# Scores computed on quarters of the TensorE array, state products moved beside the outputs, and six load buffers in place of seven

## The chip, the cores and the metric

The kernel runs on one core of one Trainium2 chip. The metric is device time in microseconds (us) of one launch. The kernel before took 572.79 us (median of three runs, 572.37 to 572.82). One further execution was profiled: 576.07 us, of which the profile's span covers 574.3 us. All durations below come from that execution.

## The reference, cut to what matters

```
scores = (q @ k.T) / sqrt(64)                  # 8 batches, 8 heads, 576 positions, head size 64
ret    = scores * D    # D[i,j] = gamma_h**(i-j) for i >= j, else 0
x      = (ret @ v), heads side by side         # 4608 tokens x 512
expert = argmax over 8 of (normalised x @ normalised expert embedding)
gate   = softmax probability of that expert
out    = gate * (relu(x @ w1[expert]) @ w2[expert])
```

The first half is a decayed causal attention without a softmax ("retention"), the second a mixture of eight experts, each token going to one of them.

## The kernel before, in words

The 4608 tokens are 36 tiles of 128. A batch has 576 positions, four and a half tiles, so nine tiles (`KT`) make two batches, and in every tile with `t % KT == 4` one batch ends after 64 rows and the next begins. The retention stage takes the decay apart into a factor of the query position and one of the key position: keys and queries are multiplied as they are, values are scaled by `gneg` (`scale_v`, on GpSimd), and results are scaled by `gsb` (`emit_X`, on VectorE). Within a tile the masked product is computed directly; what earlier tiles of the batch contribute comes from a running state per head, the sum of key times value.

Per tile t, with the names that the prediction uses:

- `emit_A(t)`, the scores: for four head pairs p and both heads h, a matmul of 64 contraction rows gives all 128 keys by 128 queries, keys on the partitions. The two heads use the upper and lower 64 rows of the array and write two banks (`pa[0:2]` for even tiles, `pa[2:4]` for odd). VectorE then multiplies each bank by a 0/1 mask (`tri`, or `trix` where a batch boundary lies inside) into `pm`.
- `emit_QT(t)`: the earlier tiles' contribution, queries times the state `T` of tile t-1, eight matmuls on 64 by 64 quarters of the array.
- `emit_O(t)`: masked scores times values, accumulated with `emit_QT` in the bank pair `po`.
- `emit_U(t)`: the state's update, accumulated in the bank `pst`; ScalarE copies it out as `T`. Where `t % KT == 4` the values come from `vx`, a copy in which the rows of the batch that ended are zero. The last tile of a batch pair needs none.
- `emit_X(t)`, `emit_T(t)`: scaled result to SBUF, and four TensorE transposes to token rows. `emit_rows` copies them (ScalarE) and stores them to the DRAM tensor `xd`; `emit_sq` sums their squares.

The stage is written by hand as 18 steps `s` (the framework doesn't reorder it): step s works on tiles t = 2s and u = 2s+1, computes the scores of the next two tiles first, and transposes the two before. Routing is strewn between: logits (`route_logits`), one-hot ranks and a table of expert slots, in a rhythm of two steps. Each engine runs its instructions in the written order and waits on semaphores.

Loads are issued on SyncE's queue (SP) in written order: 512 KB of queries and keys (`qkt`) and 512 KB of keys and values (`kvt`; only the values, 256 KB, for the first four tiles, whose keys are transposed on TensorE by `turn_k`). Each of the two has `NLOAD` buffers. At the end of a step's products the loads of tiles t+7 and u+7 are written down as qk, kv, qk, kv; each waits until its buffer's last reader is done, and all behind it in the queue wait with it. The two stores of rows stand in the same queue.

After step 17 the first expert's matmuls begin (its first three token tiles are gathered from step 14 on), and from there the mixture stage runs to the end; the change doesn't touch it.

## Time and profile before

| | |
|---|---|
| median of three runs | 572.79 us |
| profiled execution | 576.07 us, span 574.3 us |
| TensorE matmuls (PE) | 559.5 us busy, 97% |
| weight loads (PEld) | 503.1 us, 88% |
| VectorE (DVE) | 404.2 us, 70% |
| ScalarE (ACT) | 352.1 us, 61% |
| GpSimd (POOL) | 207.7 us, 36% |
| DMA queue of the loads and stores (q1) | 53.5% of 16 engines' span |

Busy time is an average over a retention stage that lasts up to about 155 us and a mixture stage behind it. In the page's 40 slices the DMA engines stand at 9 tenths or more in the first nine slices and fall to between 0 and 9 tenths afterwards, while PE stands at 9 nearly throughout. A matmul's record has a modelled end that overlaps the next, so the time of a group on PE is read here from its start to the start of the next group.

### The profile page before, as it was taken

The numbers are of one execution on the slowest core, as the hardware profiler recorded it, in microseconds if no ns is written. First come the engines' busy times: TensorE is split into PE (matmuls) and PEld (weight loads), VectorE is DVE, ScalarE is ACT, GpSimd is POOL, SyncE is SP. The second block draws the span as 40 slices with busy tenths as digits, with TensorE's granted clock in tenths as the row PEclk, the third lists the DMA queues.
The fourth block names the chain that finished last, engine by engine and source line by source line (L and its number), as shares of the span: only waits on it lengthen the run. The fifth ranks groups of instructions, "written<-read, shape, count | busy, mean of one in ns | idle before, by whom it ended". The sixth has DMA issues, their size and how long they took to land.

```text
span 574.3 us, 13123 instructions
## 1 busy us (share of the span) xinstructions
PE 559.5 (97%) x5156; PEld 503.1 (88%) x5156; DVE 404.2 (70%) x880; ACT 352.1 (61%) x640; POOL 207.7 (36%) x188
## 2 busy tenths in 40 slices
PE   8999999998999999999999999999999999999995
PEld 7888888897898889988988998898799899889985
DVE  3677678786876696787798488579868847975400
ACT  1335545554565597577778678677877856876411
POOL 4582222225634418127306602630660462070021
PEclk8999999999999999999999999999999999999999
DMA  8999999997639556835915674593576559252011
GB/s 291 405 322 337 376 337 351 384 352 191 194 112 258 129 165 178 184 93 178 279 54 165 212 147 94 171 276 59 161 251 98 140 170 245 72 174 77 2 44 43
DMA packets 83067, 111.53 MB, mean 194 GB/s; under 512 B 48135, under 2 KB 48427, under 8 KB 82992
## 3 DMA queue, kind: packets, MB, share of 16 engines
q1 hardware_dynamic: 75312, 90.55, 53.5%
q0 software_dynamic: 7680, 19.95, 10.6%
q8 instruction: 51, 0.84, 0.6%
q14 instruction: 24, 0.20, 0.1%
HBM read 81.10 MB, written 19.94 MB: 176 GB/s over the span
## 4 chain that ended last, share of the span: by engine, by line
PE 75%; issue 11%; DVE 7%; ACT 3%; POOL 1%; DMA 1%; POOLq 0%; ACTq 0%; DVEq 0%; SPq 0%
PE pa L127 27%; PE po L127 22%; PE pst L127 15%; PE prow L127 8%; PE pa L131 2%; PE prow L131 1%; DMA graw<-graw 1%; DVE graw L454 1%; POOL out L1089 1%; ACT graw L419 1%; DVE w0f L993 1%; DVE pm L662 1%; DVE hs L1022 1%; DVE st L1035 1%; ACT w0f L990 1%
## 5 line engine op out<-in xcount | busy, mean ns | idle before, releaser
L1089 POOL DMA_INDIRECT out<-y,sid x40 | 42.8, 1070 | 231.4 <-ACT y L1085 220.5
L127 PE MATMUL po<-w2f,hs 128*128 128x512 f32 x408 | 94.1, 389 | 0.0
L127 PEld LDWEIGHTS po<-w2f,hs 128*128 128x128 f32 x408 | 76.4, 188 | 15.7
L127 PE MATMUL pst<-w2f,hs 128*128 128x512 f32 (+1 forms) x336 | 78.4, 382 | 0.0
L193 DVE TENSOR_TENSOR w2f<-wraw,w2f 128x1024 fp32r<-128x1024 f32 x32 | 39.4, 1230 | 50.4 <-ACT w2f L189 40.0
L127 PEld LDWEIGHTS pst<-w2f,hs 128*128 128x128 f32 x336 | 61.0, 188 | 11.4
L645 POOL TENSOR_TENSOR kvt<-kvt,cs 128x512 f32<-128x512 f32 x35 | 37.5, 1078 | 58.3 <-DMA kvt<-kv 49.5
L398 POOL DMA_INDIRECT gt<-gd,gid x40 | 51.0, 1274 | 18.0 <-issue 11.9
L419 ACT COPY graw<-graw 128x1024 uint16<-128x1024 uint16 x37 | 50.4, 1361 | 10.3 <-DMA graw<-graw 10.3
L127 PE MATMUL pa<-xxf,w0f 128*128 128x296 f32 (+2 forms) x348 | 50.8, 296 | 1.2 <-issue 1.2
L127 PEld LDWEIGHTS pa<-xxf,w0f 128*128 128x128 f32 x348 | 47.9, 188 | 1.8 <-issue 1.5
L662 DVE TENSOR_TENSOR pm<-pa,tri 128x512 f32<-128x512 f32 x64 | 40.1, 683 | 11.9 <-PE pa L127 11.7
L127 PE MATMUL prow<-w2f,hs 128*128 128x512 f32 x192 | 46.0, 389 | 0.0
L127 PE MATMUL pa<-qkt 64*128 64x128 f32 x576 | 43.1, 286 | 0.6 <-DVE bump L266 0.4
L127 PEld LDWEIGHTS prow<-w2f,hs 128*128 128x128 f32 x192 | 36.0, 188 | 7.5
L385 POOL DMA_INDIRECT graw<-xd,gid x26 | 32.7, 1259 | 24.8 <-DVE L_all L799 14.0
L127 PEld LDWEIGHTS pa<-qkt 64*128 64x128 f32 x576 | 38.4, 192 | 3.2 <-DVE bump L266 0.6
L464 ACT CAST xxf<-graw 128x128 fp32r<-128x128 f32 x70 | 31.8, 458 | 14.0 <-DVE graw L454 12.6
L127 PE MATMUL pa<-xsf,w0f 128*128 128x296 f32 (+2 forms) x240 | 39.9, 316 | 0.1
L454 DVE TENSOR_TENSOR graw<-graw 128x128 f32<-128x128 f32 x140 | 34.4, 287 | 6.0 <-ACT graw L419 4.8
L127 PEld LDWEIGHTS pa<-xsf,w0f 128*128 128x128 f32 x240 | 36.7, 189 | 0.9 <-issue 0.4
L127 PE MATMUL po<-pm,kvt 128*64 128x128 f32 (+1 forms) x640 | 35.3, 263 | 0.3 <-issue 0.3
(196 smaller groups left out, 1105.9 us busy)
## 6 DMA issues: line engine op xcount, KB each, us to landing
wraw<-w SPq DMA_DIRECT2D x64, 512.0 KB
qkt<-qk SPq DMA_DIRECT2D x36, 512.0 KB
kvt<-kv SPq DMA_DIRECT2D x32, 512.0 KB
xd<-xw SPq DMA_DIRECT2D x36, 256.0 KB
kvt<-kv SPq DMA_DIRECT2D x4, 256.0 KB
gt<-gd,gid POOLq DMA_INDIRECT x40
out<-y,sid POOLq DMA_INDIRECT x40
graw<-xd,gid POOLq DMA_INDIRECT x26
```

The lines of the kernel that those rows point to most:

```text
L127: pe[:] = [nc.tensor.matmul(*args, **kw)]
L131: pe[:] = [nc.tensor.transpose(*args, **kw)]
L193: nc.vector.tensor_tensor(out=self.to[:, 1, c * 1024 : (c + 1) * 1024], in0=self.raws.pop(c), in1=hi.bitcast(F32), op=ALU.subtract,)
L385: return nc.gpsimd.indirect_dma_start(out=t[:, :DM].bitcast(U16), out_offset=None, in_=xd[:rows, :], in_offset=bass.IndirectOffsetOnAxis(a ...
L398: nc.gpsimd.indirect_dma_start(out=g[:, i : i + 1], out_offset=None, in_=gd[:, :], in_offset=bass.IndirectOffsetOnAxis(ap=gid[:, a : a + 1 ...
L419: copy(t[:, :DM].bitcast(U16).rearrange("p (n h) -> p h n", h=2), t[:, XO : XO + DM].bitcast(U16).rearrange("p (h n) -> p h n", h=2),)
L454: nc.vector.tensor_tensor(out=v[:, 2 * k : 2 * k + 2], in0=a, in1=b, op=ALU.subtract)
L464: nc.scalar.copy(x[:, 0], u)
L645: eng.tensor_tensor(out=v, in0=v, in1=gneg[:, t % KT].unsqueeze(2).broadcast_to([P, H, D]), op=ALU.mult)
L662: nc.vector.tensor_tensor(out=pm[:, h], in0=banks[h].rearrange("p (c n) -> p c n", c=NP), in1=m.unsqueeze(1).broadcast_to([P, NP, P]), op= ...
L990: nc.scalar.copy(wop[n][:, 0], raw[n])
L1089: sc = nc.gpsimd.indirect_dma_start(out=out[:, :], out_offset=bass.IndirectOffsetOnAxis(ap=sid[:, a : a + 1], axis=0), in_=ys[i], in_offse ...
```

## The change

Seven edits, all in the retention stage:

1. `emit_A`: each score matmul of 128 keys becomes two of 64 keys, one for each half of the output partitions. The half whose keys come first in the tile gets all 128 queries, the other only the last 64 (its first 64 queries are masked anyway). For every second head pair the host stores keys and values with their two 64-row halves swapped, so which half of the array comes first alternates from pair to pair.
2. The masks get a version for swapped pairs; `vx` and the constants follow.
3. `emit_U(t + 2)` moves from behind the transposes to right behind `emit_O(u)`.
4. At the start, `emit_U(0)` moves behind `emit_A(1)` and `turn_k(1)`, and in step 0 `emit_O(0)` goes ahead of `emit_QT(1)`.
5. `NLOAD` is 6, and a step loads tiles t+6 and u+6.
6. The four loads are written where their buffers come free: qk behind `emit_QT`, kv behind `emit_O`.
7. The 40 warm-up matmuls write all four `pa` banks, since parts of them are no longer written by scores before the mask reads them.

```diff
-NLOAD = 7
+NLOAD = 6
...
-        warm = psm.tile([P, 512], F32, name="m")
-        for _ in range(NWARM):
-            mm(warm[:, :P], one, one, start=True, stop=True)
+        for i in range(NWARM):
+            mm(pa[i % 4][:, (i // 4) % 4 * P : ((i // 4) % 4 + 1) * P], one, one, start=True, stop=True)
...
             for p in range(NP):
-                for h in range(2):
-                    hs = slice(h * D, (h + 1) * D)
-                    mm(banks[h][:, p * P : (p + 1) * P], x[hs, p, 1, :], x[hs, p, 0, :], start=True, stop=True)
+                odd = p & 1
+                for o in (odd, 1 - odd):
+                    seen = slice(0 if o == odd else D, P)
+                    for h in range(2):
+                        hs = slice(h * D, (h + 1) * D)
+                        mm(
+                            banks[h][o * D : (o + 1) * D, p * P + seen.start : (p + 1) * P],
+                            x[hs, p, 1, o * D : (o + 1) * D],
+                            x[hs, p, 0, seen],
+                            start=True,
+                            stop=True,
+                            skip_group_check=True,
+                        )
...
         emit_A(0)
         turn_k(0)
         scale_v(0, nc.vector)
-        emit_U(0)
...
         turn_k(1)
+        emit_U(0)
...
-            emit_QT(t)
+            if s == 0:
+                emit_O(t)
+            else:
+                emit_QT(t)
+            load(load_qk, t + NLOAD)
             emit_QT(u)
+            load(load_qk, u + NLOAD)
             emit_U(u)
-            emit_O(t)
+            if s > 0:
+                emit_O(t)
+            load(load_kv, t + NLOAD)
             emit_O(u)
+            load(load_kv, u + NLOAD)
...
-            if s + 1 < HS:
-                loads(t + NLOAD)
-                loads(u + NLOAD)
+            emit_U(t + 2)
...
-            emit_U(t + 2)
             emit_X(t)
```

On TensorE, around the scores of tiles 0 and 1 (`pa_73` to `pa_76` are the four banks, with keys and queries from `qkt`; the last figures are output partitions by columns), before:

```order
L127 MATMUL pa_73<-qkt 128x128
L127 MATMUL pa_74<-qkt 128x128
L131 MATMUL prow<-ident,qkt 128x128 x4
L127 MATMUL pst<-kvt 64x64 x8
L127 MATMUL pa_75<-qkt 128x128
L127 MATMUL pa_76<-qkt 128x128
```

and after:

```order
L131 MATMUL pa_73<-qkt 64x128
L131 MATMUL pa_74<-qkt 64x128
L131 MATMUL pa_73<-qkt 64x64
L131 MATMUL pa_74<-qkt 64x64
L135 MATMUL prow<-ident,qkt 128x128 x4
L131 MATMUL pa_75<-qkt 64x128
L131 MATMUL pa_76<-qkt 64x128
L131 MATMUL pa_75<-qkt 64x64
L131 MATMUL pa_76<-qkt 64x64
```

A head pair is now four matmuls on four quarters, two of 128 and two of 64 columns, and the first state product (`pst`) no longer stands between the scores of tiles 0 and 1.

On TensorE in the second half of step 1 (`po` the outputs, `pst` the state, `pa_76` and `prow` the transposes), before:

```order
L127 MATMUL po<-qkt,T 64x128 x16
L127 MATMUL pst<-kvt 64x64 x8
L127 MATMUL po<-pm,kvt 64x128 x16
L131 MATMUL pa_76<-ident,xT 128x128 x4
L131 MATMUL prow<-ident,xT 128x128 x4
L127 MATMUL pst<-vx,kvt 64x64 x8
```

and after:

```order
L131 MATMUL po<-qkt,T 64x128 x16
L131 MATMUL pst<-kvt 64x64 x8
L131 MATMUL po<-pm,kvt 64x128 x16
L131 MATMUL pst<-vx,kvt 64x64 x8
L135 MATMUL pa_76<-ident,xT 128x128 x4
L135 MATMUL prow<-ident,xT 128x128 x4
```

The second state product has moved ahead of the transposes.

On SyncE's queue in step 2, before:

```order
L541 DMA qkt<-qk 128x1024
L548 DMA kvt<-kv 128x1024
L541 DMA qkt<-qk 128x1024
L548 DMA kvt<-kv 128x1024
L772 DMA xd<-xw 128x1024 x2
```

and after:

```order
L545 DMA qkt<-qk 128x1024 x2
L552 DMA kvt<-kv 128x1024 x2
L801 DMA xd<-xw 128x1024 x2
```

The step's second query-and-key load no longer stands behind its first key-and-value load.

## Rows read from the trace of the kernel before

**Rows 1.** Windows: length, busy time of PE, PEld, DVE, ACT, POOL; PE clock, DMA share, GB/s

```profile
50.00:60.00 10.00, 10.00 (x184) 8.74 (x172) 6.15 (x19) 5.47 (x12) 3.14 (x3) 1.00 1.03 402
70.00:90.00 20.00, 20.00 (x386) 17.89 (x386) 16.12 (x40) 10.18 (x21) 6.23 (x6) 1.00 0.96 340
110.00:130.00 20.00, 20.00 (x400) 17.95 (x400) 17.27 (x40) 10.55 (x22) 4.07 (x4) 1.00 1.01 360
```

**Rows 2.** Timeline of PE (start us, length us): scores begun in steps 7 and 15

```profile
69.46 2.32 PE L127 MATMUL pa<-qkt 64*128 64x128 f32 x32
...
133.04 0.48 PE L127 MATMUL pa<-qkt 64*128 64x128 f32 x2
```

**Rows 3.** Timeline of PE: the products of steps 3, 4 and 11

```profile
36.89 2.06 PE L127 MATMUL pa<-qkt 64*128 64x128 f32 x32
38.88 1.10 PE L127 MATMUL po<-qkt,T 64*64 64x128 f32 x32
39.91 0.69 PE L127 MATMUL pst<-kvt 128*64 128x64 f32 x16
40.42 1.92 PE L127 MATMUL po<-pm,kvt 128*64 128x128 f32 x32
...
46.20 0.67 PE L127 MATMUL po<-qkt,T 64*64 64x128 f32 x16
46.80 0.69 PE L127 MATMUL pst<-kvt 128*64 128x64 f32 x16
...
103.38 0.90 PE L127 MATMUL po<-qkt,T 64*64 64x64 f32 x32
104.21 0.69 PE L127 MATMUL pst<-kvt 128*64 128x64 f32 x16
```

**Rows 4.** Timeline of PE: transposes with and without a state product behind them

```profile
107.26 0.60 PE L131 MATMUL prow<-ident,xT 128*128 128x128 f32 x4
107.79 0.69 PE L127 MATMUL pst<-kvt 128*64 128x64 f32 x16
108.41 0.19 PE L127 MATMUL pa<-oh,stri 128*128 128x32 bf16 x1
...
115.86 0.60 PE L131 MATMUL prow<-ident,xT 128*128 128x128 f32 x4
116.30 0.31 PE L127 MATMUL pa<-st 128*128 128x80 bf16 x4
```

**Rows 5.** Timelines of DVE and PE: the start, to the scores of step 2

```profile
4.71 0.29 DVE L586 TENSOR_SCALAR tri<-cs 128x128 f32<-128x128 f32 x1 [3.37 <-DMA cs<-cst]
...
8.94 1.00 PE L127 MATMUL pst<-kvt 128*64 128x64 f32 x16 [1.81 <-DVE kvt L645]
9.88 2.08 PE L127 MATMUL pa<-qkt 64*128 64x128 f32 x16
...
19.94 2.06 PE L127 MATMUL pa<-qkt 64*128 64x128 f32 x32
...
28.23 1.94 PE L127 MATMUL pa<-qkt 64*128 64x128 f32 x30
```

**Rows 6.** Window of the first 16.5 us, columns as in Rows 1

```profile
0.00:16.50 16.50, 13.76 (x168) 12.37 (x170) 4.52 (x13) 3.20 (x5) 8.89 (x16) 0.90 0.86 307
```

**Rows 7.** Timelines of SP and POOL: issue of a load, and the scaling that waits for it

```profile
106.92 0.33 SPq L548 DMA_DIRECT2D kvt<-kv  x1
114.74 1.37 POOL L645 TENSOR_TENSOR kvt<-kvt,cs 128x512 f32<-128x512 f32 x1 [1.98 <-DMA kvt<-kv]
...
128.75 0.33 SPq L548 DMA_DIRECT2D kvt<-kv  x1
```

**Rows 8.** Timelines of POOL and PE: end of step 14, step 15, scores of step 16

```profile
134.22 1.22 POOL L385 DMA_INDIRECT graw<-xd,gid  x1 [13.96 <-DVE L_all L799]
138.01 4.06 POOL L645 TENSOR_TENSOR kvt<-kvt,cs 128x512 f32<-128x512 f32 x4
...
142.67 2.41 PE L127 MATMUL pa<-qkt 64*128 64x128 f32 x32
```

## The prediction

> **What bounds the kernel now.** I read the windows first, then the timeline of TensorE (PE) through a few steps, then the queues of SyncE (SP) and GpSimd (POOL). From 70 to 90 and from 110 to 130 us PE is busy for the whole window [rows 1]: matmuls stand back to back, so a step lasts as long as its matmuls. From the scores of step 7 to those of step 15 it is (133.04 - 69.46) / 8 = 7.95 us a step [rows 2]. Two others stand close behind. The DMA engines are at a share of 0.96 to 1.03 and move 340 to 402 GB/s [rows 1]. VectorE (DVE) is busy for 17.27 of 20 us [rows 1], which is 13.7 us in the 15.9 us of two steps. So what PE is spared is gained only until a load or the mask multiplications on DVE come late.

> **Scores on quarters.** Unstalled, the two tiles' scores of a step take 38.88 - 36.89 = 1.99 us from start to start, and the two tiles' QT products behind them 39.91 - 38.88 = 1.03 us [rows 3]: 3.02 together. No row shows the new score matmul in the new alternation, but QT is the same form (64 rows by 64 columns of the array, 128 or 64 moving columns), so I price by it. One tile of QT (16 records) takes 46.80 - 46.20 = 0.60 us, two take 1.03 [rows 3]; so 16 records of 128 columns cost 0.43 us and each run of this form 0.17 once. In step 11 one of the two tiles has 64 columns and both take 104.21 - 103.38 = 0.83 us [rows 3]; less 0.17 and 0.43 that is 0.23 us for 16 records of 64 columns. A tile's new scores are 16 records of each: 0.66 us. Scores and QT now have one form and stand in one run: 0.17 + 2 x 0.66 + 0.86 = 2.35 us, 0.67 less than before. Bounds: nothing saved, if four matmuls of unlike length don't overlap as four like ones do, or even a loss (rivals below).

> The 0.17 us at the head of a QT run [rows 3] now falls away between scores and QT. [...]

> **State product beside the outputs.** Behind the transposes it costs 107.79 - 107.26 = 0.53 for the transposes in front and 108.41 - 107.79 = 0.62 for itself, against 116.30 - 115.86 = 0.44 for the same transposes without one [rows 4]: 0.71. Between QT and O, products of the same kind as its new neighbours, it costs 40.42 - 39.91 = 0.51 [rows 3]. That saves 0.20 us a step. On ScalarE the copy of the state now stands ahead of both row copies, so the bank `prow` is read sooner; nothing waits for that.

> **A step.** 0.67 + 0.20 = 0.87 us off. I take back 0.17: even now the scores of step 7 take 2.32 and not 2.06 us, since they wait until VectorE and ScalarE have read the banks they overwrite [rows 2, 3], and about 0.9 us less matmul time now lies between the transposes into `pa[3]` and the scores of tile u+2 there. VectorE's 13.7 us for two steps still fit in 14.5. So 0.70 us a step (bounds 0.3 and 0.87), a step of 7.25 us; for steps 2 to 16, 15 x 0.70 = 10.5 us.

> **The start.** PE waits 1.81 us until the values of tile 0 are scaled on VectorE, and only then does the first state product run, with the scores of tile 1 behind it [rows 5]. Now the scores of tile 1 and their transposes fill this gap, and everything up to step 1 moves forward until the queries and keys of tile 5 hold it up. What is loaded up to them is 6 x 0.524 (qk) + 4 x 0.262 + 0.524 (kv) + 0.34 (constants) = 5.06 MB; 16.5 us at 307 GB/s are 5.07 MB [rows 6], so they land at about 16.5 us. Step 1 lasted 28.23 - 19.94 = 8.29 us [rows 5]; less 0.87, and less the 0.66 of tile 4's scores, which are done before, step 2 begins at 16.5 + 8.29 - 0.87 - 0.66 = 23.3 us. On VectorE the mask constants grow by about three instructions of 0.29 us [rows 5], and the masks of tiles 4 and 5 stand behind them: 24.2 us. That is 4.0 us ahead of 28.23 (bounds 1.5 and 5).

> **Six buffers, and where the loads are issued.** A load takes up to 114.74 - 106.92 = 7.8 us from issue to the scaling that waits for it [rows 7]. In the changed kernel a qk load issued behind QT(t) is needed by the scores two steps later, 2 x 7.25 - 1.6 = 12.9 us on; a kv load, issued 2 us later, by the state product at the end of that step. So one buffer less is not felt as such. The second qk load no longer waits in the queue behind the first kv, and the row stores behind all four wait no longer than before. What counts is the rate: a step moves 4 x 0.524 + 2 x 0.262 = 2.62 MB, in the four steps with an expert weight block 3.15 MB. At 402 GB/s [rows 1] that is 6.5 and 7.8 us against 7.25 us. The four long ones are 2.3 us over, the others have 0.7 us each to spare. I take a loss of 1.7 us (bounds 0 and 9; by the 402, since that window has stores and a weight block in it too).

> **POOL's queue in step 15.** The scaling of tiles 32 to 35 stands behind three gathers, which wait for the routing table: from 1.18 us after the step's first scores, the first scaling ends 138.01 + 1.02 - 133.04 = 6.0 us after them [rows 2, 8]. The state product of tile 32, moved forward, wants it about 1.9 (scores with their waits) + 0.8 + 0.5 + 1.9 = 5.1 us after them. PE, and all behind it, waits 0.8 us (bounds 0 and 1.5). In the kernel before, that product came behind the transposes and was covered.

> **Sum.** 4.0 + 10.5 - 1.7 - 0.8 = 12.0 us, against the profiled execution's 576.07 us (span 574.3 and 1.8 around it): 564.1. The median of the runs is 3.3 us lower, 572.79, so I expect 560.8 us. Everything behind step 17 hangs on the last rows and moves as a whole.

> **Rivals.**
> - *Loads become the bound.* For: a DMA share of 1.01 at only 360 GB/s, 0.96 at 340 [rows 1]. Against: 402 at 1.03. Up to the last load 36 x 0.524 (qk) + 34 x 0.524 (kv) + 30 x 0.262 (stores) + 4 x 0.524 (weights) + 0.34 = 47.0 MB move, 41.9 of them after 16.5 us. At 350 GB/s the last lands at 16.5 + 119.7 = 136.2 us, and the scores of tiles 34 and 35, at 142.67 before [rows 8], start then: 6.5 us, and 0.5 in the rest: 565.8 us (563 at 360, 569 at 340 GB/s). The last kv was issued at 128.75 [rows 7], so even this leaves a gain: PE didn't need it so early.
> - *Quarters in lockstep.* A group of four goes only when its longest is through: 16 groups of 0.43 / 4 = 0.1075 us are 1.72 us for two tiles, the run 2.75, the step 0.27 + 0.20 - 0.17 = 0.30 us shorter. 15 x 0.30 + 3.6 - 0.8 = 7.3 us: 565.5. No row has lengths that alternate; the order of halves, turned from pair to pair, speaks against it, as the half with 64 columns is the next pair's first. [...]
> - *VectorE becomes the bound.* Its 13.7 us for two steps need 0.8 us of waits to reach 14.5. For: in every second step masks, one-hots and the weight split stand in one chain. Against: it waits for PE between them. With half the gain, 0.35 us a step, and 0.6 us for loads, 5.3 + 4.0 - 0.8 - 0.6 = 7.9: 564.9 us.
> - *Slower: only two quarters run at a time.* Then a tile's scores are the eight pairs of before (0.91 us) and eight of half the length (0.45): 2.72 us for two tiles, and the run 0.17 + 2.72 + 0.86 = 3.75, 0.73 longer. A step grows by 0.73 - 0.20 + 0.17 = 0.70, 15 x 0.70 = 10.5; the start keeps 1.3, POOL's wait stays: 572.8 + 10.5 - 1.3 + 0.8 = 582.8 us. It decides from a pair of scores of 2.3 us on. Against it: QT already runs its 16 records in 0.43 us, half of what the wide form takes.

> **How the numbers follow.** Forecast 0.48; loads 0.18; lockstep 0.17; VectorE 0.10; two at a time 0.07. The forecast's own range is 557 to 564 us. Loads, lockstep and VectorE lie between 563 and 569, so 556 to 568 us leaves out the slower case, the slowest loads and a step that loses its full 0.87: under 2 in 10. Faster by over 0.2% (about what a measurement of this kernel can tell from no change): 0.91; within it 0.02; slower 0.07.

> **What would show it.** In the profile of the changed kernel: scores of two tiles in 1.3 to 1.6 us from start to start (1.7 or more is lockstep, 2.3 or more two at a time), QT right behind; a state product of 0.51 us behind the outputs; scores of step 2 at 24 us; steps 7 to 15 at 7.2 to 7.3 us on average; a PE wait of under 1 us for scaled values in step 15. Idle time of PE before scores that ends with `qkt`'s landing would show the loads as the bound, waits for `pm` before the outputs VectorE. The prediction is wrong if the step has its shorter scores and the mixture stage still doesn't begin 10 us or more sooner.

## The result: 4.1 us slower, not 12 us faster, and the profile after

The changed kernel takes 575.76 us (median of 14 runs, 572.81 to 578.97), the kernel before 571.63 us beside it (14 runs, 570.52 to 573.38): ratio 1.0064, 95% interval 1.0044 to 1.0084. The forecast was 560.8 us, with a range of 556 to 568. Both profiled executions took 576.07 us. That is the changed kernel's median, but some 4 us above that of the kernel before; a second profile of each was taken later.

Windows of the changed kernel, columns as in [rows 1]:

```profile
16.50:30.00 13.50, 10.28 (x206) 9.73 (x209) 7.83 (x19) 2.89 (x7) 6.63 (x11) 0.75 0.88 321
70.00:90.00 20.00, 17.45 (x455) 15.51 (x448) 15.98 (x40) 10.73 (x23) 5.35 (x5) 1.00 0.97 343
110.00:130.00 20.00, 18.47 (x463) 16.25 (x463) 18.38 (x43) 12.43 (x25) 5.12 (x6) 1.00 0.96 360
```

TensorE was busy for the whole of two of these windows [rows 1]; now it is idle for 1.5 to 2.6 us of each 20, and DMA share and GB/s are about what they were. In the first window the granted clock is at its lower level (0.5 in the profile's rows, against 1.0) from 19.06 to 25.89 us; it fell while TensorE waited 3.22 us, until 20.49, for the queries and keys of tile 5. The matmuls did become shorter. This is the PE timeline of a step of the changed kernel without a stop, to the next scores, and the same step of the kernel before:

```profile
77.91 2.00 PE L131 MATMUL pa<-qkt 64*64 64x128 f32 x60
79.69 0.27 PE L131 MATMUL po<-qkt,T 64*64 64x128 f32 x1
79.73 0.29 PE L131 MATMUL pa<-qkt 64*64 64x64 f32 x4
79.81 1.09 PE L131 MATMUL po<-qkt,T 64*64 64x128 f32 x31
80.82 1.97 PE L131 MATMUL po<-pm,kvt 128*64 128x128 f32 x32
82.62 0.63 PE L131 MATMUL pst<-kvt 128*64 128x64 f32 x16
83.18 1.08 PE L131 MATMUL pa<-xT,E 128*32 128x128 f32 x32
...
85.50 0.43 PE L131 MATMUL pa<-qkt 64*64 64x128 f32 x2
```

```profile
76.98 2.41 PE L127 MATMUL pa<-qkt 64*128 64x128 f32 x32
...
85.30 0.87 PE L127 MATMUL pa<-qkt 64*128 64x128 f32 x8
```

7.59 us against 8.32: 0.73 less, where 0.70 was forecast. The state product takes 83.18 - 82.62 = 0.56 us. But such a step is the exception. PE's waits from 14 to 150 us (total, times, longest), the changed kernel and then the one before:

```profile
PE po L131 <- issue: 5.3, 6, 1.5
PE pa L131 <- DMA qkt<-qk: 3.2, 1, 3.2
PE pa L131 <- DVE tab L359: 2.4, 3, 1.1
PE pa L131 <- DVE t L299: 1.4, 2, 1.0
PE pa L131 <- issue: 0.9, 3, 0.5
PE pst L131 <- issue: 0.9, 1, 0.9
```

```profile
PE pa L127 <- issue: 0.9, 1, 0.9
PE po L127 <- issue: 0.9, 3, 0.4
```

"issue" is a wait for nothing that the profile names, in the middle of a run of equal products. One of them, in PE's timeline, and the DMA queues in the 0.2 us from 71.1 to 71.3 us:

```profile
71.10 0.76 PE L131 MATMUL po<-qkt,T 64*64 64x128 f32 x18
73.36 0.66 PE L131 MATMUL po<-qkt,T 64*64 64x128 f32 x13 [1.50 <-issue]
```

```profile
q8 instruction: 1, 0.02, 30.0%
```

A packet of the instruction queue starts there, and 2.2 us later TensorE goes on. The pages' rows of that queue for the whole execution, after and before, say how large a packet is:

```profile
q8 instruction: 55, 0.90, 0.6%
```

```profile
q8 instruction: 51, 0.84, 0.6%
```

The traces have 14308 instructions of all engines after and 13123 before; over 55 and 51 packets that is 260 and 257 each, in 16 KB. Between stops on TensorE lie one or more times 256 matmuls and weight loads. The windows from stop to stop in the changed kernel (34.16, 39.92; 90.60, 97.25; 107.80, 113.78):

```profile
34.16:39.92 5.76, 5.40 (x127) 4.48 (x127) 3.35 (x10) 3.42 (x7) 4.88 (x8) 1.00 0.93 320
90.60:97.25 6.65, 5.54 (x129) 4.91 (x129) 4.38 (x13) 4.25 (x8) 1.32 (x2) 1.00 0.97 357
107.80:113.78 5.98, 5.43 (x128) 4.80 (x129) 3.55 (x11) 3.47 (x8) 0.00 (x0) 1.00 0.96 339
```

From the records, a block's packet starts 0.5 to 4.7 us after TensorE has entered the block ahead of it (2.7 on average from 14 to 150 us; 2.4 in the kernel before), and its instructions run 2.2 us after that at the earliest. Before, 256 instructions lasted 6.8 us on average, so the next block was there in time but for two stops of over 0.3 us (1.8 us together). Now they last 5.8, and of 23 blocks 11 came late, by 10.0 us together. A step has 363 instructions instead of 299 (recorded matmuls and weight loads of steps 7 and 8, halved), so it uses up 1.42 blocks instead of 1.17. Without their stops 256 of them would last 5.77 - 10.0 / 23 = 5.3 us on average, and a packet that starts later than 5.3 - 2.2 = 3.1 us into the block ahead makes TensorE wait (an estimate from these means; single blocks differ). A step is now (143.27 - 29.36) / 14 = 8.14 us between the scores of steps 2 and 16, where 7.25 was forecast.

### The profile page after: what moved, and what is told of

It reads as the page before. It is cut to its first block, busy times and chain, and to the rows that moved or that the text cites. A ratio compares the mean times of both kernels' runs of the same rounds, so it can differ in the third digit from the quotient of the medians.

```text
span 574.3 us, 14308 instructions
## 1 busy us (share of the span) xinstructions
PE 548.4 (95%) x5732; PEld 495.1 (86%) x5732; DVE 409.2 (71%) x882; ACT 354.6 (62%) x640; POOL 209.2 (36%) x192
## 3 DMA queue, kind: packets, MB, share of 16 engines
q0 software_dynamic: 7680, 19.95, 10.5%
HBM read 81.10 MB, written 19.94 MB: 176 GB/s over the span
## 4 chain that ended last, share of the span: by engine, by line
PE 64%; issue 13%; DVE 11%; DMA 5%; ACT 3%; POOL 2%; SPq 0%; POOLq 0%; ACTq 0%; DVEq 0%
PE pa L131 23%; PE po L131 18%; PE pst L131 14%; PE prow L131 7%; DMA qkt<-qk 3%; DVE graw L458 2%; PE pa L135 1%; DMA graw<-graw 1%; DVE pm L691 1%; POOL out L1122 1%; DVE w0f L1026 1%; DMA graw<-xd,gid 1%; DVE xT L779 1%; DVE hs L1055 1%; PE prow L135 1%
## 5 line engine op out<-in xcount | busy, mean ns | idle before, releaser
L402 POOL DMA_INDIRECT gt<-gd,gid x40 | 50.4, 1260 | 19.4 <-issue 11.9
L773 ACT COPY T<-pst 128x256 f32<-128x256 f32 x32 | 11.9, 373 | 60.3 <-PE pst L131 60.1
L131 PE MATMUL pa<-qkt 64*64 64x64 f32 (+1 forms) x1152 | 37.2, 254 | 9.6 <-DMA qkt<-qk 4.3
L131 PEld LDWEIGHTS pa<-qkt 64*64 64x64 f32 x1152 | 29.8, 136 | 15.7 <-DVE entry L613 3.3
L468 ACT CAST xxf<-graw 128x128 fp32r<-128x128 f32 x70 | 31.7, 458 | 13.7 <-DVE graw L458 13.4
L131 PE MATMUL po<-pm,kvt 128*64 128x128 f32 (+1 forms) x640 | 37.0, 266 | 2.7 <-issue 2.7
```

What stands on the lines that cost most here:

```text
L131: pe[:] = [nc.tensor.matmul(*args, **kw)]
L402: nc.gpsimd.indirect_dma_start(out=g[:, i : i + 1], out_offset=None, in_=gd[:, :], in_offset=bass.IndirectOffsetOnAxis(ap=gid[:, a : a + 1 ...
L468: nc.scalar.copy(x[:, 0], u)
L773: nc.scalar.copy(T, u[:, :NP])
```

## The experiments

Theory A: TensorE's instructions arrive too late. Theory B: VectorE frees the score banks too late. Theory C: six buffers, the loads' new places or the new start cost it. "Block-end stops" below are those of 0.3 us or more between 14 and 150 us, from the start of a block's last instruction to the start of the next block's first; so they are longer than the idle times in the lists of waits, and a wait for another engine at such a place is in them too. The start of the mixture stage is that of its first product on TensorE: 155.59 and 154.20 us in two profiles of the kernel before, 156.25 and 161.37 of the changed one. Each ratio is to runs of the kernel before on the same chip; times and profiles of different runs are mostly of different chips, on which the kernel before takes 571.0 to 575.0 us.

**Each part alone, on the kernel before.**

```
e1_quarters: emit_A on quarters, with the masks, gneg and the inputs' layout that go with it
e1_loads:    NLOAD = 6; load_qk(t+6) behind emit_QT(t), load_kv(t+6) behind emit_O(t)
e1_start:    emit_U(0) behind turn_k(1); in step 0 emit_O(t) in place of emit_QT(t)
e1_state:    emit_U(t + 2) behind emit_O(u), ahead of emit_T
```

> The kernel before with the scores on quarters alone (seven buffers, loads, start and state product as before). Theory A, TensorE's instruction supply: the quarters add 32 matmuls and 32 weight loads a step, and the run of them stops for the next block of instructions; gaps without a semaphore of 0.5 to 1.8 us stand 1 to 2 us behind the 16 KB packets of the instruction queue, some 5 to 9 us in all up to 150 us, so of the 10 us that shorter matmuls spare at most half is left: 567 to 571 us against 571.6. Theory B, VectorE comes late for the score banks: the gaps before scores are 0.7 to 1.3 us in the even steps, 4 to 5 us in all: 566 to 568. Theory C, the six buffers and the new places of the loads cost it: here they are as before, so the whole 0.67 us a step shows, 561 to 563.

> The kernel before with six load buffers and each load handed out where one comes free, nothing else. Theories A and B: no change, within 1 us of before. Theory C: 5 us or more slower, with waits of TensorE for qkt and a second fall of its clock.

> The kernel before with the order of the first two tiles changed alone (scores and transposes of tile 1 ahead of the first state product, outputs of tile 0 without the QT product). By the prediction: up to 4 us faster at the scores of step 2. If tile 5's queries and keys are what the start waits for, as the trace of the changed kernel shows (they landed at 20.4 us and TensorE waited 3.2 us and then ran at half clock): within 1.5 us of before.

> The kernel before with the state product moved beside the outputs alone. By its price in the trace, 0.20 us a step: 3 us faster. Theory B: it stands ahead of the transposes, so these and all that VectorE does with them come 0.5 us later; 0 to 1 us faster. Theory A says the same as the price: 3 us.

Measured: quarters 579.93 us (ratio 1.0134, 1.0092 to 1.0176), loads 571.38 (0.9978 to 1.0017), start 571.13 (0.9966 to 1.0003), state product 567.08 (0.9923, 0.9896 to 0.995). So the slow part is the one whose matmuls became shorter, and C is out as the cause. A was nearest for the quarters, though its 567 to 571 us were 9 us too low: the block-end stops are 16.7 us where 5 to 9 were expected, and after two of them (to 50.02 and 68.02 us) the granted clock falls to its lower level for 3.4 us each (0.76 on average from 48 to 55 us, 0.74 from 66 to 72.5). The longest stop, in the PE timeline of the quarters alone, 2.3 us behind a packet:

```profile
107.81 0.46 PE L131 MATMUL po<-pm,kvt 128*64 128x64 f32 x9
110.76 1.51 PE L131 MATMUL po<-pm,kvt 128*64 128x64 f32 x34 [2.49 <-issue]
```

**Same instructions, less traffic, and the control without quarters.**

```
 def load_qk(t):
+    if t >= NLOAD:
+        qkt[t] = qkt[t - NLOAD]
+        return
```

> The changed kernel without the loads of queries and keys from tile 6 on (the buffers of the first six tiles are read again, so the scores are those of other tiles): same instructions on every engine, 1.05 MB a step less to load. Theory A, TensorE runs dry at the end of each 256 instructions, since the next 16 KB of them start 3 to 4 us late behind the loads and are usable 2.2 us after that: the packets start within 1.5 us of the last block's end, the gaps at the block ends (9.4 us from 14 to 150 us in the changed kernel) shrink under 2 us, and the time falls by 6 to 9 us to 567 to 570. Theory B, VectorE late for the score banks (0.7 to 1.3 us in front of scores in even steps): gaps there as before, time within 2 us of the changed kernel's 575.8. Theory C, loads late by themselves: as A for the time, but the gaps that vanish are those that end with a landing of qkt, of which the changed kernel has one only, at 20.5 us.

> The changed kernel without quarters (568.3) and without the loads of queries and keys from tile 6 on, as in the half-traffic run (scores of other tiles). With quarters that gave 9.1 us. Theory A: TensorE has 299 instructions a step here and rarely runs dry (2.5 us of block-end gaps with the full traffic), so less traffic gives 1 to 3 us: 565 to 567, and both half-traffic kernels come out alike or the one with quarters (566.7) ahead. If less traffic helps by other ways (VectorE, the start, row stores): 5 us or more here too, 560 to 563.

Measured: with quarters 566.71 us (0.988 to 0.9921), 9.1 us below the changed kernel; without, 574.26 where before is 574.95 (0.9967 to 1.0021), against 0.994 with the full traffic. The totals hold more than the loop: behind the first mixture product these two take 421.7 and 423.8 us to the end, all others 416 to 419; that the other scores change the routing is likely, but wasn't tried. In the loop itself the answer is plain. The mixture stage begins, with quarters, at 143.99 instead of 156.25 and 161.37 us, and without them at 148.59 instead of 149.32. The 148.59 hold some 1.7 us of the short stops that are told last in this document, in step 15; from the scores of step 2 to those of step 15 it is 97.5 instead of 106.1 and 110.7 us with quarters, and 100.7 instead of 102.9 without. So the kernel without quarters gains 2.2 us, which is what its block-end stops took, and the one with quarters 8.6 and 13.2, of which its stops make 6.7 and 10.1. The packets' mean delay falls from 2.7 to 1.6 us with quarters and from 2.4 to 0.6 without, the block-end stops from 10.0 to 4.0 (A had said under 2) and from 2.2 to 0. PE's waits of the half-traffic run with quarters:

```profile
PE po L131 <- issue: 1.8, 3, 0.8
PE pa L131 <- DVE tab L359: 1.2, 3, 0.5
PE pa L131 <- DVE t L299: 1.0, 1, 1.0
```

Theory A is shown: same instructions, earlier packets, fewer stops, and no more gain in the control than its own stops. Of B some 2 us stay: in front of scores TensorE waits 2.6 us for VectorE here, and 4.7 with the full traffic.

**More instructions without shorter work.**

```
-for h in range(2):
-    mm(banks[h][:, p*P:(p+1)*P], x[hs, p, 1, :], x[hs, p, 0, :], ...)
+for o in range(2):
+    for h in range(2):
+        mm(banks[h][:, p*P+o*D : p*P+(o+1)*D], x[hs, p, 1, :], x[hs, p, 0, o*D:(o+1)*D], ...)
```

> The kernel before with each score matmul cut in two of 64 moving columns each, on the same 64 by 128 form: as many matmuls and weight loads more as the quarters bring (32 and 32 a step in the records), the same work for the array, nothing left out. Theory A: the blocks of 256 instructions are used up sooner than they arrive, gaps without a semaphore at their ends of 8 us or more from 14 to 150 us, and the time at least 8 us above 571.6, that is 580 or more, even if the halves cost no more on the array. Theory B: nothing but what the halves cost on the array; gaps at the block ends stay at 2 us, 571 to 574.

Measured: 606.39 us (ratio 1.0621), with a single stop at a block's end, of 0.3 us. A's number is met for a reason that neither theory had: a product of half the columns took as long as one of all of them.

```profile
82.35 4.05 PE L127 MATMUL pa<-qkt 64*128 64x64 f32 x64
86.33 1.10 PE L127 MATMUL po<-qkt,T 64*64 64x128 f32 x32
```

3.98 us for 64 of these, 1.99 for 32 of twice the columns [rows 3]. Each product brings a weight load of its own (1152 of each in the trace); whether that or the product sets the time wasn't tried. With the scores' time doubled, a block lasts long enough (6.8 us on average) for the next one to arrive. As a test of A this is void.

**The other parts without quarters; the weight split moved.**

```
e2_no_quarters: the changed kernel with emit_A, masks and rows as before
e2_split_late:  at((8 + 2*i, 1), ...) -> at((9 + 2*i, 1), ...)
```

> The changed kernel with the scores on the whole width as before (state product beside the outputs, start and loads as changed). The three other parts alone gave 4.6, 0.5 and 0.3 us. Theory A: their sum, 566 to 567. Theory C (the six buffers and the start cost when the step is shorter): 570 or more, with the 3.2 us wait for tile 5 at the start.

> The changed kernel with the first weight split of the loop (high and low half on VectorE and ScalarE) moved from the even steps to the odd ones, away from the routing. Theory B: the waits of 0.7 to 1.3 us in front of scores in steps 6, 10 and 14 fall to 0.3, and the time by 3 to 4 us to 572. Theory A: TensorE then reaches the end of a block sooner and waits there instead; the time within 1.5 us of 575.8.

Measured: without quarters 568.28 us (0.9924 to 0.9956), 1 to 2 us short of the gain that the sum had; with the split moved 580.03 (1.0134 to 1.0192). There B predicted 572 and A 574.3 to 577.3, and both missed. The waits that were meant did go: in front of the scores of steps 5, 9 and 13 (6, 10 and 14 as the expectation counts) the changed kernel has 0.5, 1.05 and 0.99 us, and this one none over 0.2. But TensorE, spared them, stops at the next block's end: 14.8 us of these instead of 10.0. And at 146.5 us a new wait for VectorE of 4.5 us came, about as long as this kernel is slower than the changed one. So sparing TensorE those waits gained nothing, as A said; the new wait is the edit's own.

**Fewer buffers, other loads.**

```
e3_five_buffers:   NLOAD = 6 -> 5
e3_quarters_state: e1_quarters with e1_state, seven buffers
e3_start_state:    e1_start with e1_state, seven buffers
```

> The changed kernel with five load buffers: fewer loads stand in the DMA queues at once. If the instruction packets' delay (2.7 us on average in the changed kernel, 1.6 with half the traffic) goes with what is queued ahead of them, it falls to 2 us or less and the time to 570 or below, unless loads then come late for the scores (waits for qkt, 580 or more). If it goes with the share of the DMA engines' time, which stays at 0.93 to 0.98, no change: within 2 us of 575.8.

> The changed kernel with seven buffers, the loads where they were and the old start: quarters and state product alone. If the handed-out loads help the instruction packets through (delay 3.1 us on average with quarters alone, 2.7 in the changed kernel): above 575.8, 576 to 579, with more than 9.4 us of gaps at the block ends. If the six buffers and the start cost the changed kernel anything: below 574.

> The kernel before with the state product beside the outputs and the new order of the start, seven buffers and loads as before. If the parts add up: 571.6 - 4.6 - 0.5 = 566.5. It and the state product alone (567.1) are what the versions with quarters must beat.

Measured, in this order: 582.81 us (1.0172 to 1.0227), 575.27 (1.0057 to 1.0117) and 567.38 (0.9918 to 0.9964). With five buffers the packets are as late as before (2.75 us) and loads come late too: PE waits 8.8 us for qkt, 6.7 of them at once. With quarters and seven buffers the stops are 12.6 us, and the time falls into neither of the two expected ranges. Buffers and order of the loads decide little there; the two good parts without quarters don't add beyond the state product alone.

**Quarters for one tile of the two.**

```
 for p in range(NP):    # e3_one_tile: quarters if t is even; e4_second_tile: if t is odd
     mm(banks[h][:, p*P:(p+1)*P], x[hs, p, 1, :], x[hs, p, 0, :], ...)   # the other tile
```

> The changed kernel with only the first tile of each step on quarters; the second tile's scores run on the whole width with the same layout and masks. Theory A: a step has 331 instructions on TensorE instead of 363, at 5.6 us for 256 (the mean of the blocks of the changed kernel from 14 to 150 us is 5.77, of the half-traffic run 5.27) 7.25 us, under the 7.4 us that its matmuls take; so the block ends stop being the bound, the gaps there fall from 9.4 to 3 to 5 us, and half of the quarters' 10 us is left: 563 to 566. If every added instruction costs in proportion instead: between no quarters (568.3) and all (575.8), 572. Theory B: the waits for VectorE stay, 570 to 573.

> The changed kernel with only the second tile of each step on quarters (the first tile's scores wide). With the first tile alone on quarters the scores of a step took 2.18 and 2.30 us, against 2.25 and 2.34 with none: the second tile's scores wait there until ScalarE has squared the rows in bank 3 and VectorE has read bank 1. If these reads set the start of the second tile's scores, quarters in the second tile shorten the step by 0.33 to 0.38 us, and 331 instructions a step still arrive in time: scores in 1.9 to 2.0 us, block-end gaps of 2 to 4 us, 563 to 565. If what counts is the number of instructions alone: as with the first tile, 570.

> The same with seven buffers and the loads where they were (start and state product as changed; without quarters this gave 567.4). Same gain of 0.33 to 0.38 us a step: 562 to 564; with more delay of the instruction packets than with the loads handed out (3.1 against 2.7 us with all scores on quarters), 564 to 567.

Measured: 570.11 us (0.9971 to 1.0026), 568.17 (0.9922 to 0.9967) and 569.16 (0.9944 to 0.9998). None is better than no quarters at all. The gains that were expected of A's reasoning were missed in all three; only the first lies in a stated range, at the edge of theory B's 570 to 573. The stops are down, to 1.8 us with the first tile on quarters and 4.6 with the second, but the gain is gone too. ScalarE and PE of the first-tile run show why:

```profile
74.13 2.37 PE L131 MATMUL pa<-qkt 64*64 64x128 f32 x48
74.60 0.60 ACT L809 ACTIVATE st<-pa 128x512 bf16<-128x512 f32 x1
75.09 0.20 ACT L809 ACTIVATION_READ_ACCUMULATOR st<-pa 128x1 f32 x1
76.43 1.10 PE L131 MATMUL po<-qkt,T 64*64 64x128 f32 x32
```

The second tile's scores overwrite `pa[3]`, which ScalarE reads until 75.29 us (they start at 75.32); shorter scores of the first tile only wait for that. Scores of a step take 2.18 and 2.30 us, against 2.25 and 2.34 without quarters. With the second tile on quarters they are 2.07 and 2.17, not the 1.9 to 2.0 expected, and the stops take the rest.

**Second profiles.**

> The kernel before, for a second profile: its first one was taken of an execution of 576.07 us, 4 us over its median. If those 4 us lay in the start or in block-end gaps, they are gone here: first products of the mixture stage at 151 to 153 us instead of 155.6.

> The changed kernel, for a second profile. In the first, TensorE waited 3.2 us for the queries and keys of tile 5 at 20.5 us and then ran at the lower clock for 6.8 us, so that step 2 began at 29.4 us. If that is what the new start does, it is seen again, step 2 at 28 to 30 us; if it was one straggling load of one execution, the wait is about 1 us as in the versions with quarters (0.7 to 1.0 us), step 2 at 26 to 27 us. Block-end gaps of 9 to 15 us from 14 to 150 us in either case.

Measured: 575.07 us beside a median of 574.95 on that chip, and 580.74 beside 574.76. In the kernel before, the mixture stage begins at 154.20 us; the expected 151 to 153 was missed. The 1.4 us gained lie ahead of step 2, whose scores begin at 26.83 instead of 28.23: in the first profile the granted clock was at its lower level from 9.12 to 12.53 us, behind the wait for the first scaled values [rows 5], and in the second it doesn't fall (1.00 over the first 16.5 us and the 13.5 us behind them). A window of the first profile, columns as in [rows 1]:

```profile
10.00:12.00 2.00, 2.00 (x17) 1.78 (x18) 0.01 (x1) 0.36 (x1) 2.00 (x4) 0.50 1.05 398
```

In the changed kernel, tile 5 is waited for again, for half as long, and the clock doesn't fall there (1.00 from 16.5 to 30 us); step 2 starts at 26.66 instead of 29.36 us. The stops are 13.7 us. Its mixture stage still begins 5.1 us later than in the first profile. After a block-end stop to 33.03 us the clock is at its lower level for 3.4 us, and step 2 lasts 11.4 us; in step 15, after a series of short stops, it is there again for 3.4 us, and the step lasts 11.9 (0.91 on average from 30 to 50 us and from 130 to 150). Its PE timeline, and that of the first profile:

```profile
19.85 0.90 PE L131 MATMUL pa<-qkt 64*64 64x128 f32 x32 [1.54 <-DMA qkt<-qk]
...
26.66 0.79 PE L131 MATMUL pa<-qkt 64*64 64x128 f32 x26
```

```profile
20.49 1.56 PE L131 MATMUL pa<-qkt 64*64 64x128 f32 x32 [3.22 <-DMA qkt<-qk]
21.80 1.96 PE L131 MATMUL po<-qkt,T 64*64 64x128 f32 x32
...
29.36 0.90 PE L131 MATMUL pa<-qkt 64*64 64x128 f32 x30
```

Of the versions that compute the right scores, the fastest is the kernel before with the state product alone moved: 567.08 us, 0.8% under before and 1.4% under the changed kernel (0.9923 / 1.0064). The one with the new start as well, 567.38, can't be told from it.

## Why the prediction was wrong, point by point

- **The step that failed** stands in the first paragraph of the reasoning: PE is busy, "so a step lasts as long as its matmuls", with DMA and VectorE the only ones close behind. A third stood closer, the supply of instructions, and the change adds a fifth to what a step needs of it (299 to 363). So what the shorter matmuls spared came back as waiting at the ends of blocks: 11 of 23 blocks came late, by 10.0 us together, and a step took 8.14 us instead of the forecast 7.25. The kernel before showed the sign of it: 256 instructions in 6.8 us against a delay of up to 3.9 plus 2.2 us, and two stops already. It was not a rival. The prediction's own test came out against it: the scores are shorter, and the mixture stage doesn't begin 10 us sooner.
- **Quarters, 0.67 us a step, less 0.17 for late banks.** The mechanism held. In step 2 of the changed kernel, where nothing is late, the two tiles' scores take 30.74 - 29.36 = 1.38 us, and the run of scores and QT 31.53 - 29.36 = 2.17, against 31.05 - 28.23 = 2.82 before. One of these two QT tiles has 64 columns, so the prediction's prices give 0.17 + 2 x 0.66 + 0.43 + 0.23 = 2.15. So the 0.17 is paid once in the run, as the prediction had it, and not a second time where the operand changes (2.32). The changed kernel and the one before:

```profile
29.36 1.57 PE L131 MATMUL pa<-qkt 64*64 64x128 f32 x64
30.74 0.85 PE L131 MATMUL po<-qkt,T 64*64 64x64 f32 x32
31.53 0.69 PE L131 MATMUL pst<-kvt 128*64 128x64 f32 x16
```

```profile
28.23 2.06 PE L127 MATMUL pa<-qkt 64*128 64x128 f32 x32
30.21 0.90 PE L127 MATMUL po<-qkt,T 64*64 64x64 f32 x32
31.05 0.69 PE L127 MATMUL pst<-kvt 128*64 128x64 f32 x16
```

  Lockstep (1.72 us) and two at a time (2.72) are refuted for these lengths. Behind a wait, 58 of the 64 ran in 1.24 us:

```profile
53.40 1.46 PE L131 MATMUL pa<-qkt 64*64 64x128 f32 x58 [0.52 <-DVE tab L357]
54.64 0.27 PE L131 MATMUL po<-qkt,T 64*64 64x128 f32 x1
```

  The 0.17 was too small: in the steps without a stop or a named wait the scores take 1.62 or 1.79 us, 0.3 to 0.5 over the 1.32 of the forecast. For the second tile's bank the row of ScalarE above shows the reader that they wait for; for the rest it is likely the same, but wasn't shown. Over 13 steps the half-traffic runs take 97.5 us with quarters and 100.7 without, 0.25 a step less; with the remaining stops of the one with quarters (some 2.6 us in these steps) taken off, it is 0.45 against the 0.50 forecast.
- **State product, 0.20 a step.** This was right, if anything too low: moved alone, it gave 4.6 us (2.9 to 5.9) against 15 x 0.20 = 3.0.
- **Start, 4.0 us.** This was wrong. Alone it gave 0.5 us, and in the changed kernel step 2 began at 29.36 and 26.66 us, not 24.2. The landing of tile 5 was put at 16.5 us by the mean rate; TensorE got it at 20.49 and 19.85. A mean rate says when the last byte of all could arrive, not when this load does. And the 28.23 us that the gain was counted from held a fall of the clock: with the old start, step 2 begins at 26.83 us in the second profile, at 26.35 in that of the loads alone and at 25.20 in that of the state product alone, against 25.48 with the new start alone. So little of the 4.0 was there to gain, and some 1.4 of it were taken off twice, since the 3.3 us between the profile and the median were taken off too (as far as the median run has no such fall).
- **Loads, 1.7 us lost.** Nothing was lost: alone they cost nothing, and in the loop (from step 2 on) no scores waited for qkt. The rival of the loads as the bound was wrong for the data, though what the loads do delay is the instructions.
- **POOL in step 15, 0.8 us.** The prediction's own terms give 6.0 - 5.1 = 0.9. The wait can be seen where nothing else is late: with half the traffic the state product of step 15 waits 0.5 us for the scaled values. In the first profile of the changed kernel it doesn't.
- **VectorE.** This rival had the right place. In front of scores PE waits 4.7 us for it from 14 to 150 us, and 0.9 before. It is the smaller part.
- **The sum.** First profile against first profile, to the start of the mixture stage: block-end stops +8.2 (10.0 against 1.8), VectorE in front of scores +3.8, the start +1.1 (29.36 against 28.23), a series of short stops that only the kernel before had, -1.7 (told below), and 14 steps of the forecast's 0.87 us less matmul time, -12.2, make -0.8. Measured is +0.7 (156.25 against 155.59). The 1.5 us left over are 0.1 a step. Late banks can be the reason, since the one step without a stop shown above was 0.73 shorter, not 0.87; this wasn't followed through all steps.

## What to carry to other kernels

Before cutting a matmul in more and shorter ones, divide the instructions of a stage by the block that the stops and packets show (256 in this case), multiply by the time that a block takes to come under the traffic of that stage (here 2.2 us and a delay of 2.7 on average and up to 4.7), and compare with the stage's time. Here that makes 1.42 x 4.9 = 7.0 us on average and 1.42 x 6.9 = 9.8 at most, against a forecast step of 7.25 (an estimate from these runs), and the changed kernel without quarters, with fewer instructions, was faster (0.994 of before) than the one with shorter matmuls (1.0064). A PE that was 97% busy before didn't show this; waits with "issue" as the releaser in the middle of a run of equal products, 2.2 us behind a packet of the instruction queue, did. And where shorter products overwrite a bank, price the reader of the bank first.

## What the runs showed of the hardware that was not expected

- With more load traffic an instruction packet of 16 KB started later after TensorE had entered the block ahead: on average 0.6 us with half the traffic and no quarters (226 GB/s from 30 to 140 us) and 1.6 with quarters (232 GB/s), 1.9 to 3.1 in the runs with the full traffic (342 GB/s in the changed kernel). Whether it stands behind queued loads or shares the DMA engines' time with them stays open; five buffers instead of six, which queue fewer loads, changed nothing (2.75 us).
- On the 64 by 128 form a product of 64 columns took what one of 128 did (0.062 us each: 3.98 us for 64, 1.99 for 32). On the 64 by 64 form 64 products, half of them of 64 columns, took 1.38 us (0.022 each) in step 2 of the changed kernel, and the short ones did gain: 64 of 128 columns at QT's price of 0.43 for 16 would be 1.72.
- Open: in both profiles of the kernel before, in that of the half-traffic run without quarters and in the second of the changed kernel, PE stops some three to five times in a row in step 15, for 0.2 to 0.4 us every 0.73 us, at no block's end and with nothing named. In the second profile of the changed kernel:

```profile
139.86 0.47 PE L131 MATMUL pa<-qkt 64*64 64x128 f32 x5 [0.39 <-issue]
140.63 0.46 PE L131 MATMUL pa<-qkt 64*64 64x64 f32 x5 [0.30 <-issue]
141.36 0.42 PE L131 MATMUL pa<-qkt 64*64 64x128 f32 x5 [0.27 <-issue]
```

Between two of them run about ten matmuls and weight loads. In the first three the step is 1.7 to 1.9 us longer by it (9.45 to 9.81 us instead of 7.8 to 7.95). In the fourth the granted clock is at its lower level right after it, from 143.58 us for 3.4 us. The cause wasn't looked into.
